# Joining the first layer's feature tiles in threes, with the block's order written out by hand

## The chip, the cores and the metric

The kernel runs on one core of a Trainium2 chip. The metric is the device time of one execution in microseconds (us), the median of several runs. A profile of one execution gives the time of each instruction on the engines: TensorE (PE, its weight loads shown apart as PEld), VectorE (DVE), ScalarE (ACT), GpSimd (POOL) and SyncE (SP), which here issues the transfers.

## What is computed

An RWKV6 attention (4 sequences, 8 heads of 48 dimensions, 768 tokens) feeds a two-layer network on 3072 tokens:

```python
for t in range(S):                                   # attention, per sequence and head
    cur = np.einsum('bhd,bhe->bhde', u[None] * kt, vt)
    y[:, :, t] = np.einsum('bhd,bhde->bhe', rt, state + cur)
    state = wt[:, :, :, None] * state + np.einsum('bhd,bhe->bhde', kt, vt)
...
h = x @ w_in                 # x: 3072 x 384 (the attention's results), w_in: 384 x 2048
g = h - np.tanh(h)
return g @ w_out             # w_out: 2048 x 384
```

## The kernel before

The tokens are worked on in 8 blocks of 384 (two for each sequence). A block's x lies transposed in three tiles of 128 x 384 (`xT`), and the 2048 features are 16 tiles of 128. For each feature tile there are four steps:

- the first layer: h = w_in x into PSUM, either plain (`first`, L899: three products of 128 x 384 columns) or joined (below);
- `slight` (L977), which makes g: on ACT two tanh of h with different scales and a square (L987, L988, L991), on DVE a product of the two results (L905). These three activations are called a slot below;
- forms of g: the second layer of a pair of tiles is done with 15 products of 128 x 128 in place of 18 for each 128 tokens (`Fewer`, L1082). It needs ten sums and differences of parts of g, made two at a time by `form_g` (L1006, DVE, 128 x 256 each, five per pair). Some forms read the one made just before;
- the products (L1096): twelve go into three PSUM accumulators (`acc`), three "odd" ones into `hp`. At the end of a block, twelve sums on DVE (`sum`, L1124 and L1132) turn the 15 accumulated results into the output, which goes out from `sums`.

The joined first layer of blocks 2 to 7 is `Twos` (L911): two feature tiles by 11 products of 192 columns (half of the block's tokens, L961) in place of 12. Weight forms (`kept`) are made once (L937); four token forms for each block (`turned`, L945) are differences of parts of x. One ACT copy (L962) and four additions on DVE (L971) for a pair make h in `joint`. In block 2 three of the eight pairs are joined, in blocks 3 to 6 six, in block 7 seven; the other tiles are plain.

Beside this runs the attention of the next block. For each block and half of the heads there are, in this order: running products of the decays (L431, L443), their products with k and r (L450, L457), splitting into 16-bit parts and transposing (ACT copies L556 and L566), scores of earlier tokens on PE (L508) with masked copies out of PSUM on DVE (`earlier`, L516), the state update on PE (L589) and DVE (L601), the results (`together`, L785) and ACT's copies of them into xT (L757), and a bound on the size of exponents (`bound`, L474, ACT, 128 x 780).

Each engine works through its instructions in the order in which the program wrote them. For the work around a tile f the program writes: the first layer's products, `slight`, then the list `ops` on DVE (the product of the tile before, forms, attention work, sums, mixed one by one by `between`), then what `due` says of the second layer's products, some tiles later. `plan(i)` says at which tile each piece of the attention stands. `EMPTY` counts empty instructions strewn between PE's products.

Of the kernel before, what the change touches and what calls it, by code (L numbers as in the profile page):

```python
# [37 lines left out]
F32 = mybir.dt.float32  # L38
# [81 lines left out]
TWOS = range(7)  # L120
BESIDE = (0, 1, 2, 3, 4, 7)
EMPTY = (159, 0, 92, 0, 16, 0, 40, 0)
JOINED = {2: (1, 4, 7), 3: BESIDE, 4: BESIDE, 5: BESIDE, 6: BESIDE, 7: TWOS}
PAIRS = range(0, 1), range(1, 2), range(2, 3), range(3, 5), range(7, 8)
LEFT = range(5, 7)
FORMED = {(1, 8): (1, (0, 2, 1, 4, 3)), (2, 5): (4, (0, 2, 1, 4, 3)), (2, 6): (3, (0, 2, 1, 4, 3)),
          (2, 12): (0, (0, 2, 1, 4, 3)), (2, 13): (2, (0, 2, 1, 4, 3)),
          (6, 12): (5, (0, 2)), (6, 13): (5, (1, 4, 3))}
# [8 lines left out]
def kernel(  # L137
# [59 lines left out]
    def draw(names, cols):  # L197
        nc.gpsimd.memset(mask_all[0:L, cols], 1.0)
        for m in names:
# [5 lines left out]
            else:  # L205
# [13 lines left out]
    states = [states0[:, 0:NPAIR * NCH * L].rearrange("d (p c e) -> d p c e", c=NCH, e=L),  # L219
              const.tile([P, NPAIR, NCH, L], F32, name="states1", tag="states1")]  # L220
# [13 lines left out]
    def g_at(q, x):  # L234
        if not isinstance(x, str):
            return 6 + q % 2 * 4 + x if x < 4 else 10 + x
        return (q % 2 * 3 if x[1] == "a" else 20 + q % 4 * 3) + int(x[0])

# [40 lines left out]

    class Kept:  # L280

        def __init__(self, pool):
            self.both, self.n = [pool.tile([P, 2, BANK], F32, name=f"att{j}", tag=f"att{j}") for j in range(2)], 0

        def tile(self, *_, **__):
            self.n += 1
            return self.both[self.n % 2]

    class Turns:
# [4 lines left out]
        def tile(self, *_, **__):  # L296
            self.n += 1
            return self.tiles[(self.n - 1) % len(self.tiles)]
# [8 lines left out]
    def scratch(ps):  # L307
        return ps.tile([P, 2, BANK], F32, name="att", tag="att")
# [19 lines left out]
    kept = const.tile([P, 5 * len(BESIDE) * P], F32, name="kept", tag="kept")  # L328
    turned = const.tile([P, 2 * NB], F32, name="turned", tag="turned")
    joint = const.tile([P, 6 * HB], F32, name="joint", tag="joint")  # L330
# [3 lines left out]
    class Block:  # L334
# [87 lines left out]
        def begin(self):  # L422
            self.xT = [xpool.tile([P, NB], F32, name=f"xT{i}", tag=f"xT{i}") for i in range(KC)]
            self.late = None
            return self.xT
# [62 lines left out]
        def gram(self, ps, lhs, rhs, p0, n, m=None, spare=0, ahead=0, late=0):  # L488
# [7 lines left out]
            used = ps_t[:, :, 0:n * NCP * width]  # L496
            gr = used.rearrange("s h (p c t) -> s h p c t", p=n, c=NCP)
            for p in range(p0, p0 + n):
                for c in range(NCP):
                    for h in range(2):  # L500
                        for par in range(2):
                            rows = slice(64 * h, 64 * h + D)
                            src = self.chunk(rhs, p, 2 * c + par, rhs == "pre" and not m)[rows]
                            dst = gr[64 * par:64 * par + 64, h, p - p0, c, :]
                            if m:
# [3 lines left out]
                                                         start=True, stop=True)  # L509
                            self.opened = self.opened or self.done  # L510
            return used

        def masked(self, ps, lhs, rhs, mask, p0, **fill):
            gr = self.gram(ps, lhs, rhs, p0, UP, **fill)
            mask = mask.bitcast(U8).unsqueeze(1).unsqueeze(1)
            return lambda x=0, n=UP: nc.vector.copy_predicated(  # L516
                out=A[:, :, p0 + x:p0 + x + n].rearrange("s h p c t -> s h (p c) t"),
                mask=mask.to_broadcast([P, 2, n * NCP, L]),
                data=gr[:, :, x * NCP * L:(x + n) * NCP * L].rearrange("s h (n t) -> s h n t", t=L))
# [15 lines left out]
        def turn_2(self, p0):  # L535
            ks = self.keys()[:, p0:p0 + UP]
            nc.scalar.copy(out=ks.rearrange("t p c d -> t p (c d)"), in_=self.turned_as[:, :, 0:NCP * P])
# [35 lines left out]
        def update_1(self, ps):  # L573
            last, wide = self.q == NQ - 1, D if isinstance(ps, Kept) else L
            for cs in ((0, 1), (2,)):
                kvp = scratch(ps)
# [3 lines left out]
                for p in reversed(range(NPAIR)):  # L580
                    for c in cs:
                        for h in range(2):
                            for par in range(2):
                                if last and 2 * c + par == NCH - 1:
# [6 lines left out]
                                                 rhs=self.v[toks, c, e0:e0 + D], start=True, stop=True)  # L591

        def update_2(self):
# [9 lines left out]
            if self.q > 0:  # L603
                step(St[:, :, 0, 0:D], St[:, :, 0, 0:D], tot(0), ALU.mult)
            for c in range(NCH - 1 if self.q == NQ - 1 else NCH):
                dst = St[:, :, c + 1, 0:D] if c + 1 < NCH else states[self.q + 1][:, :, 0, 0:D]
                kv = self.kv[c].rearrange("d (p e) -> d p e", e=D)
# [138 lines left out]
        def result_out(self, pairs, copy=None):  # L746

            copies = []
            for p in reversed(pairs):
# [3 lines left out]
                src = self.yp[p % 2][:, :, n * NCP * L:(n + 1) * NCP * L].rearrange("e a (c t) -> e c a t", t=L)  # L753
                dst = self.xT[p] if p < KC else self.late
                dst = dst.rearrange("e (c a t) -> e c a t", a=2, t=L)
                for h, rows in enumerate((slice(0, D), slice(64, 64 + D)) if copy else (slice(0, P),)):
                    copies.append((copy[h] if copy else nc.scalar.copy)(out=dst[rows], in_=src[rows]))  # L757
            return copies[0]

        def together(self, ps):  # L760
# [34 lines left out]
            for of in (from_state, scores) if self.q else (scores, from_state):  # L795
                for cross in range(2):
                    stretch(of, cross)
            self.result_out(ALL, None if spread else [nc.scalar.copy] * 2)
# [9 lines left out]
        def phase(self, ps, name):  # L808

            if name in ("own", "earlier"):  # L810
# [41 lines left out]
        def level(self, ps, m, p0, n):  # L852
            gr = self.gram(ps, "post", "pre", p0, n, m)
# [54 lines left out]
    def spare_tile(name, width=2 * HALF, pool=inp):  # L908
        return pool.tile([P, width], F32, name=name, tag=name, bufs=1)

    class Twos:  # L911
# [3 lines left out]
        def __init__(self):  # L915
            self.forms, self.sets, self.to = {}, [], []

        def form(self, pairs, tiles):
            tiles = [t.rearrange("p (j c) -> p j c", c=P) for t in tiles]
            self.sets.append((pairs, tiles))  # L920
            for n, j in enumerate(pairs):
# [696 lines left out]
```

## Time and profile before

| | |
|---|---|
| median of 3 runs | 537.41 us (536.76 to 539.31) |
| the profiled execution | 535.64 us |
| its span, first to last instruction | 533.9 us |
| granted TensorE clock | 0.999 |
| busy time of PE, DVE, ACT | 523.9, 478.1, 312.4 us |
| first token form of blocks 2, 4, 5, 7 | 152.5, 276.5, 339.2, 463.9 us |

Shares of the span are busy shares: PE 98%, DVE 90%, ACT 59%. Lines such as L961 are lines of the kernel before; those of the changed kernel are other numbers. In the profile's rows stand the start, the duration, the engine, the line, the operation, the tile written and the tiles read, the shape and the number of instructions in the row; the time in brackets is how long the engine had been idle, with what ended that. "128x384" is 128 partitions by 384 columns.

### The profile page before, as it was taken

How to read it: one execution, taken by the hardware profiler on the slowest of the kernel's cores; microseconds unless marked ns; L12 is line 12 of the kernel's file. 1: busy time of each engine (PE TensorE's matmuls, PEld its weight loads, DVE VectorE, ACT ScalarE, POOL GpSimd, SP SyncE). 2: the span in 40 equal slices, each digit the busy share in tenths (PEclk: the TensorE clock that was granted, in tenths of full speed). 3: DMA queues.
4: the chain of work that ended last, by engine and by line, in shares of the span. 5: the costliest groups of instructions: out<-in, count | busy, mean ns of one | idle time of the engine just before them, and what ended most of it. 6: DMA issues, size and time to landing. Idle time of an engine off the chain costs nothing.

```text
span 533.9 us, 14969 instructions
## 1 busy us (share of the span) xinstructions
PE 523.9 (98%) x6040; PEld 449.2 (84%) x6040; DVE 478.1 (90%) x1011; ACT 312.4 (59%) x729; POOL 9.1 (2%) x57
## 2 busy tenths in 40 slices
PE   7999999999999999999999999999999999999996
PEld 5756665677887879999799998999889997999994
DVE  7999996698889999999999999999999999667874
ACT  4999984665536473655646375375735655454350
POOL 1100000000000000000000000000000000000001
PEclk9999999999999999999999999999999999999999
DMA  8799632352312452035420832145321430200011
GB/s 282 258 406 342 224 120 71 107 132 64 122 26 72 104 143 95 0 89 166 120 58 2 192 119 66 54 66 142 108 88 31 79 116 1 58 1 1 10 36 48
DMA packets 53048, 56.35 MB, mean 106 GB/s; under 512 B 21488, under 2 KB 50928, under 8 KB 52976
## 3 DMA queue, kind: packets, MB, share of 16 engines
q1 hardware_dynamic: 52592, 55.18, 34.7%
q8 instruction: 49, 0.80, 0.6%
q14 instruction: 23, 0.19, 0.1%
q10 hardware_dynamic: 288, 0.10, 0.1%
q0 software_dynamic: 96, 0.07, 0.1%
HBM read 44.73 MB, written 4.72 MB: 93 GB/s over the span
## 4 chain that ended last, share of the span: by engine, by line
PE 83%; DVE 13%; issue 2%; DMA 1%; SPq 0%; DVEq 0%
PE acc L1096 23%; PE att L961 20%; PE hp L899 17%; PE acc L1047 6%; PE hp L1096 5%; PE att L785 3%; DVE g L1010 2%; PE att L508 2%; DVE joint L971 2%; DVE g L905 1%; PE att L589 1%; DVE pre L431 1%; PE acc L1074 1%; PE att L1096 1%; PE att L899 1%
## 5 line engine op out<-in xcount | busy, mean ns | idle before, releaser
L1096 PE MATMUL acc<-forms,g 128*128 128x128 f32 x972 | 135.5, 276 | 0.0
L1096 PEld LDWEIGHTS acc<-forms,g 128*128 128x128 f32 x972 | 124.3, 192 | 3.8
L899 PE MATMUL hp<-xT,w_sb 128*128 128x384 f32 x330 | 116.5, 489 | 0.0
L1010 DVE TENSOR_TENSOR g<-g 128x256 f32<-128x256 f32 x270 | 110.5, 418 | 6.1 <-DVE g L1010 0.5
L899 PEld LDWEIGHTS hp<-xT,w_sb 128*128 128x128 f32 x330 | 59.5, 190 | 33.3
L905 DVE SCALAR_TENSOR_TENSOR g<-h,qa 128x384 f32<-128x384 f32 x112 | 61.7, 551 | 18.1 <-ACT h L991 17.9
L987 ACT ACTIVATE h<-joint 128x384 f32<-128x384 f32 x54 | 27.9, 517 | 77.5 <-DVE joint L971 77.5
L961 PE MATMUL att<-xT,w_sb 128*128 128x192 f32 x340 | 72.0, 326 | 0.0
L987 ACT ACTIVATE h<-hp 128x384 f32<-128x384 f32 x55 | 27.2, 495 | 58.5 <-PE hp L899 58.4
L991 ACT ACTIVATE h<-h 128x384 f32<-128x384 f32 x113 | 58.2, 515 | 0.0
L961 PEld LDWEIGHTS att<-xT,w_sb 128*128 128x128 f32 x340 | 56.4, 190 | 0.0
L971 DVE TENSOR_TENSOR joint<-joint,att 128x384 f32<-128x384 f32 (+1 forms) x108 | 51.6, 499 | 4.9 <-PE att L961 3.0
L1096 PE MATMUL acc<-w_sb,g 128*128 128x128 f32 x324 | 54.5, 277 | 0.0
L1096 PEld LDWEIGHTS acc<-w_sb,g 128*128 128x128 f32 x324 | 45.9, 192 | 4.4
L961 PE MATMUL att<-turned,kept 128*128 128x192 f32 x192 | 36.5, 327 | 0.1
L1132 DVE TENSOR_TENSOR sums<-sums 128x256 f32<-128x256 f32 x84 | 33.3, 410 | 1.4 <-ACT sums L1109 0.9
L1047 PE MATMUL acc<-w_sb,sums 128*128 128x384 f32 x96 | 33.7, 487 | 0.0
L272 ACT ACTIVATE up<-raw 128x768 f16<-128x768 f32 (+1 forms) x32 | 33.0, 1108 | 0.0
L961 PEld LDWEIGHTS att<-turned,kept 128*128 128x128 f32 x192 | 32.0, 190 | 0.4 <-DVE turned L945 0.4
L1096 PE MATMUL hp<-w_sb,g 128*128 128x128 f32 x176 | 29.5, 275 | 0.0
L1047 PEld LDWEIGHTS acc<-w_sb,sums 128*128 128x128 f32 x96 | 18.1, 190 | 12.3
L988 ACT ACTIVATE qa<-joint 128x384 f32<-128x384 f32 x54 | 27.5, 509 | 0.0
(157 smaller groups left out, 795.5 us busy)
## 6 DMA issues: line engine op xcount, KB each, us to landing
raw<-in_weights SPq DMA_DIRECT2D x16, 768.0 KB, 7.4
w<-in_wT SPq DMA_DIRECT2D x7, 780.0 KB, 4.4
k<-in_kT SPq DMA_DIRECT2D x7, 768.0 KB, 4.6
r<-in_rT SPq DMA_DIRECT2D x7, 768.0 KB, 4.5
v_sb<-in_v SPq DMA_DIRECT2D x8, 576.0 KB, 5.1
k<-in_tokens SPq DMA_DIRECT2D x7, 576.0 KB, 4.1
r<-in_tokens SPq DMA_DIRECT2D x7, 576.0 KB, 4.2
out_y<-sums SPq DMA_DIRECT2D x18, 128.0 KB, 1.9
```

Source lines behind the costliest of these rows:

```text
L272: return lambda: nc.scalar.activation(out=to, in_=of, func=AF.Copy, scale=scale, bias=bias)
L899: nc.tensor.matmul(hp, lhsT=w_in_sb[:, f, kc, :], rhs=xT[kc], start=(kc == KC - 1), stop=(kc == 0))
L905: return lambda: nc.vector.scalar_tensor_tensor(out=out, in0=in0, scalar=scalar, in1=in1, op0=op0, op1=ALU.mult)
L961: nc.tensor.matmul(to, lhsT=lhs, rhs=rhs, start=n == 0, stop=n + 1 == len(of))
L971: return [lambda of=of: nc.vector.tensor_tensor(out=of[0], in0=of[1], in1=of[2], op=ALU.add) for of in ((h[:, 0:5:4], twice(h[:, 3]), both ...
L987: made = nc.scalar.activation(out=t, in_=h, func=AF.Tanh, scale=INNER / UPSCALE)
L988: nc.scalar.activation(out=by, in_=h, func=AF.Tanh, scale=OUTER / UPSCALE)
L991: nc.scalar.activation(out=t, in_=t, func=AF.Square, accum_out=top[:, n:n + 1])
L1010: return lambda: nc.vector.tensor_tensor(out=G[:, to:to + 2], in0=two(G, g_at(q, a0), g_at(q, a1)), in1=two(G, g_at(q, b0), g_at(q, b1)), ...
L1047: nc.tensor.matmul(acc, lhsT=g[:, j * P:(j + 1) * P], rhs=w_out_sb[:, f, :], start=(f == self.first), stop=(f == NF - 1))
L1096: nc.tensor.matmul(to, lhsT=G[:, g_at(q, a), :], rhs=rhs, start=start, stop=stop, skip_group_check=True)
L1132: ops.append(lambda op=op, at=at: nc.vector.tensor_tensor(out=at[0], in0=at[1], in1=at[2], op=OPS[op]))
```

## The change

`Twos` becomes `Threes` (L961 of the changed kernel): in blocks 2 to 7 three feature tiles are made by 15 products of 192 columns in place of 18, in five triples (tiles 0 to 2, 3 to 5, 6 to 8, 10 to 12, 13 to 15); tile 9 (`LONE`) is plain, and in block 7 so are tiles 13 to 15. Two sets of running sums lie in four PSUM banks, and some sums are to be used at two stages. So the products stop at stages where ACT copies a sum out with its sign changed (a "tap", L1047: three between the stages and at the end, four of 384 columns and one of 192 for each triple), into SBUF or into another bank where the next products are added. After the last tap six additions on DVE (L1050) give h of three tiles.

```diff
+        def begin(self, banks, f0, between, fill):
...
+            products((3, sums[0]), (5, sums[1]), start=3)
+            between(0)
+            tap(both(1), both(0, True))
+            products((0, singles[0]), (12, singles[1]), start=0)
+            fill(0)
+            products((2, chain[0]), (11, chain[1]))
+            between(1)
+            tap(T[:, 3:7:3], both(1))
+            products((8, sums[0]), (14, sums[1]), (13, apart_sums[0]), start=13)
+            fill(1)
+            products((10, chain[0]), (7, chain[1]))
+            between(2)
+            tap(T[:, 5], apart_sums[0])
+            tap(T[:, 0:5:4], both(1))
+            products((9, apart_sums[1]), (4, apart_sums[0]))
+            fill(2)
+            products((6, chain[0]), (1, chain[1]))
+            tap(T[:, 1:3], both(1))
+            between(3)
+            adding(T[:, 4:7], T[:, 1:4], T[:, 4:7], "add")
+            adding(T[:, 1], singles[0], T[:, 1], "sub")
+            adding(T[:, 0:3:2], both(0), T[:, 0:3:2], "add")
+            adding(T[:, 4:7:2], both(2), T[:, 4:7:2], "sub")
+            adding(T[:, 5], T[:, 5], T[:, 1], "sub")
+            adding(T[:, 1], singles[1], T[:, 1], "add")
```

`between(n)` writes at stage n the slot of a tile of the triple before and lists for ACT and DVE (A, V), `fill(n)` gives PE second-layer products. Eleven of the fifteen products use weight forms, in all 55 tiles of 128 columns: too many to keep. They are made in blocks 0 and 1 (17 operations on 384 columns for three triples, 17 on 256 for two; L993, L994), written to memory (`drawn`), and read back for each triple in three parts into one area (`ring`, 11 x 128 columns, 720 KB). The token forms of a block are six operations (L1016: four of 384 columns, two of 192).

The order of blocks 2 to 7 is written out by hand: a period for each triple, with the pieces of the attention, the forms, sums and loads at fixed places.

```diff
+        def between_stages(n):
+            if n < 3:
+                if waiting:
+                    ins, ops = slot(n)
+                    made.append(ins)
+                else:
+                    ops = []
+                run(A[n])
+                run(V[n] + ops)
+            else:
+                run(A[3])
+        def fill(n):
+            pull((3, 1, 2)[n])
+            run(fills[n])
+        threes.begin(banks, TRIPLES[t], between_stages, fill)
...
+        period(2, [form(fewer, 0, 1), form(fewer, 1, 0) + sums_of[:4], sums_of[4:] + form(fewer, 1, 1),
+                   form(fewer, 2, 0) + of(later, "diagonal_in 2", "diagonal_in 0")],
+               [[], [lambda: phase("join 0 0")], [lambda: phase("join 0 1")], [lambda: phase("join 0 2")]],
+               [[], [], [lambda: odd(fewer, 0)]], tail_2)
+        h = first(blk.xT, LONE, banks[1][:, 0:NB])
+        chain = later.update_2(True) if later else []
+        waiting.insert(0, (i, LONE, h))
+        made, ops = slot(0)
+        run(form(fewer, 2, 1) + chain[:2] + ops)
+        pull(6)
+        def tail_3(made):
+            load(after, "r", made)
+            pull(6)
+            odd(fewer, 2)
+            if later:
+                ps_a.n = 0
+                later.together(ps_a, None)
+                later.result_by_bank()
+                later.fill_holes([nc.sync])
...
+        period(4, [form(fewer, 4, 0), of(after, "behind 0", "take_whole 0") + form(fewer, 4, 1), of(after, "before 2"),
+                   form(fewer, 5, 0) + [lambda: run(threes.token_forms(later.x))]],
+               [[], [lambda: after and after.bound(HALVES[0])], [lambda: after and after.bound(HALVES[1])], []],
+               [[], [], [lambda: odd(fewer, 3)]], tail_4)
```

`pull(n)` writes the next n of the second layer's products (L1198) that are due; `odd` writes a pair's three odd products, which now add up over all eight pairs, so that the sum of two halves (L1124) goes. Also changed: the state update is copied out of PSUM by ACT (`update_out`, five copies), the results go out in eight copies of 192 columns by PSUM bank (`result_by_bank`, L807), masked copies of 768 columns become two of 384, g has 41 tiles of room in place of 32, and `EMPTY` is 275 in place of 307.

The order on DVE in a middle block before, around the additions of a pair (L971), with the forms L1010:

```order
L971 TENSOR_TENSOR joint<-joint,att_128 128x2x192
L1010 TENSOR_TENSOR g<-g 128x256
L971 TENSOR_TENSOR joint<-joint,att_127 128x2x192
L971 TENSOR_TENSOR joint<-joint,att_127 128x192
L971 TENSOR_TENSOR joint<-joint,att_127 128x384
L457 TENSOR_TENSOR post<-k,post 128x768
L1010 TENSOR_TENSOR g<-g 128x256
L457 TENSOR_TENSOR post<-k,post 128x768
L1010 TENSOR_TENSOR g<-g 128x256
L450 TENSOR_TENSOR pre<-r,pre 128x12x64
L1010 TENSOR_TENSOR g<-g 128x256
```

and on DVE now, in period 0, with the token forms L1016, the forms L1112 and the products L1098:

```order
L1016 TENSOR_TENSOR area<-xT 128x384
L1016 TENSOR_TENSOR area<-area,xT 128x384 x2
L1016 TENSOR_TENSOR area<-xT,area 128x384
L1016 TENSOR_TENSOR area<-xT,area 128x192
L1016 TENSOR_TENSOR area<-area 128x192
L1112 TENSOR_TENSOR g<-g 128x256 x3
L467 TENSOR_TENSOR post<-k,post 128x768
L460 TENSOR_TENSOR pre<-r,pre 128x12x64
L1098 TENSOR_TENSOR g<-h,qa 128x384
L1112 TENSOR_TENSOR g<-g 128x256 x2
L440 RECIPROCAL start<-whole 128x12
L441 SCALAR_TENSOR_TENSOR pre<-w,start 128x780
```

The forms that stood singly between other work now stand in twos and threes. On PE before, the products of a pair and those of the second layer behind it:

```order
L961 MATMUL att_128<-xT_1894,w_sb 128x192
L961 MATMUL att_128<-xT_1895,w_sb 128x192
L961 MATMUL att_128<-xT_1896,w_sb 128x192
L961 MATMUL att_128<-turned,kept 128x192
L961 MATMUL att_127<-turned,kept 128x192 x2
L961 MATMUL att_127<-xT_1896,w_sb 128x192
L961 MATMUL att_127<-xT_1895,kept 128x192
L961 MATMUL att_127<-xT_1896,kept 128x192
L961 MATMUL att_127<-turned,w_sb 128x192
L961 MATMUL att_127<-xT_1896,w_sb 128x192
L1096 MATMUL acc_133<-forms,g 128x128 x4
```

and on PE now, most of a triple in period 3 (the banks att_598 to att_601):

```order
L1028 MATMUL att_598<-area,w_sb 128x192
L1028 MATMUL att_598<-area 128x192
L1028 MATMUL att_601<-area,w_sb 128x192
L1028 MATMUL att_601<-xT,area 128x192
L1198 MATMUL acc_126<-forms,g 128x128 x2
L1198 MATMUL acc_596<-w_sb,g 128x128
L1028 MATMUL att_599<-area,w_sb 128x192
L1028 MATMUL att_599<-area 128x192
L1028 MATMUL att_598<-xT,area 128x192 x2
L1028 MATMUL att_600<-xT,area 128x192
L1198 MATMUL acc_596<-forms,g 128x128
L1028 MATMUL att_599<-area 128x192 x2
```

The products of a triple stand in pairs with the second layer's between them. On ACT before, the results' copies (L757) with the slots around them:

```order
L987 ACTIVATE h<-hp 128x384
L988 ACTIVATE qa<-hp 128x384
L991 ACTIVATE h,top<-h 128x384
L757 COPY outward_118<-att_128 128x384
L757 COPY xT_1315<-att_127 128x384
L757 COPY xT_1314<-att_128 128x384
L757 COPY xT_1313<-att_127 128x384
L987 ACTIVATE h<-hp 128x384
```

and on ACT now, from period 3 to period 4, with the copies L807, the slots L1088 and L1093, and the first tap L1047:

```order
L807 COPY xT<-att_598 128x3x64 x2
L807 COPY xT<-att_599 128x3x64 x2
L807 COPY outward_118<-att_600 128x3x64
L807 COPY xT<-att_600 128x3x64
L807 COPY outward_118<-att_601 128x3x64
L807 COPY xT<-att_601 128x3x64
L1088 ACTIVATE h<-area 128x384
L1088 ACTIVATE qa<-area 128x384
L1093 ACTIVATE h,top<-h 128x384
L1047 ACTIVATE att_599<-att_598 128x384
L1088 ACTIVATE h<-area 128x384
```

The copies stand ahead of the first slot, and the tap that the products wait for stands behind it.

607 lines of the change are left out of this document (369 added, 238 removed).

## The prediction

> **What bounds the kernel now.** I read the page first (busy line, share of the chain, waits), then the windows from one start of a block's token forms to the next, then the chain inside a middle block, then the rows of VectorE (DVE) and ScalarE (ACT) for prices. The page's busy line, its chain by engine, and from the waits of DVE the largest:
>
> ```profile
> PE 523.9 (98%) x6040; PEld 449.2 (84%) x6040; DVE 478.1 (90%) x1011; ACT 312.4 (59%) x729; POOL 9.1 (2%) x57
> PE 83%; DVE 13%; issue 2%; DMA 1%; SPq 0%; DVEq 0%
> DVE g L905 <- ACT h L991: 17.9, 18, 2.0
> ```
>
> TensorE (PE) carries the end, but DVE is busy 90% of the time. By block this is sharper. The windows are: start-up and blocks 0 and 1, two middle blocks, the last block; after the length come the busy times of PE, its weight loads, DVE, ACT, POOL, then the granted clock and the DMA share.
>
> ```profile
> 0.00:152.52 152.52, 148.55 (x1818) 103.33 (x1819) 132.69 (x247) 109.96 (x209) 5.49 (x33) 1.00 0.55 187
> 276.48:339.19 62.71, 62.71 (x767) 58.62 (x767) 60.37 (x129) 35.76 (x92) 0.32 (x4) 1.00 0.36 92
> 339.19:401.50 62.31, 62.31 (x766) 58.27 (x765) 60.12 (x129) 35.74 (x92) 0.32 (x4) 1.00 0.37 93
> 463.87:533.90 70.03, 65.35 (x456) 60.78 (x455) 50.29 (x128) 29.33 (x82) 2.17 (x6) 0.99 0.07 21
> ```
>
> A middle block takes 62.3 us, PE has no idle time in it, and DVE only 2.2 us. So PE bounds it by a hair: what is taken from PE can shorten a block by about 2 us, unless DVE's work shrinks too. The change does the opposite.
>
> [...]
>
> The chain, for PE's prices (an entry counts weight loads and matmuls, so x22 is 11 products):
>
> ```profile
> 291.65 1.74 PE att L508 x96
> ...
> 294.93 3.58 PE att L961 x22
> 298.50 2.68 PE acc L1096 x24
> ...
> 318.39 1.43 PE att L589 x80
> ...
> 321.35 1.94 PE hp L899 x6
> ...
> 327.90 2.83 PE att L785 x192
> ...
> 525.63 2.62 PE acc L1074 x8
> ```
>
> Hence 3.58/11 = 0.326 us for a product of 192 columns, 2.68/12 = 0.2235 for one of 128 columns in the second layer, 1.94/3 = 0.646 for one of 384 columns in the first; 1.74 for the scores of the earlier tokens, 1.43 for the state updates, 2.83 for the attention's results.
>
> DVE's rows:
>
> ```profile
> 344.92 0.55 DVE L971 TENSOR_TENSOR joint<-joint,att 128x384 f32<-128x384 f32 x1
> 345.39 0.42 DVE L1010 TENSOR_TENSOR g<-g 128x256 f32<-128x256 f32 x1
> 345.72 1.40 DVE L971 TENSOR_TENSOR joint<-joint,att 128x384 f32<-128x384 f32 x3
> 347.04 0.95 DVE L457 TENSOR_TENSOR post<-k,post 128x768 f32<-128x768 f32 x1
> 347.91 0.42 DVE L1010 TENSOR_TENSOR g<-g 128x256 f32<-128x256 f32 x1
> ...
> 355.23 1.97 DVE L516 COPY_PREDICATED scores<-mask_all,att 128x768 f32<-128x768 uint8 x2
> 357.09 0.41 DVE L1010 TENSOR_TENSOR g<-g 128x256 f32<-128x256 f32 x1
> ...
> 364.51 1.48 DVE L1010 TENSOR_TENSOR g<-g 128x256 f32<-128x256 f32 x3
> 365.91 0.55 DVE L905 SCALAR_TENSOR_TENSOR g<-h,qa 128x384 f32<-128x384 f32 x1
> ```
>
> Durations overlap, so I count from start to start: 0.47 us for 384 columns (344.92 to 345.39), 0.33 for 256 (345.39 to 345.72), 0.87 for 768, and by that slope 0.27 for 192 and 0.67 for 576. Two masked copies of 768 take 1.86, thus about 0.5 for half of one. The last pair matters most: three second-layer forms (L1010) in a row, each reading the one before, take 1.40 (364.51 to 365.91), where three that stand apart take 3 x 0.33 = 1.0. A form right behind the form that it reads costs about 0.2 more, and I take 0.12 (an operation that waits for one thing) to 0.19 (for two).
>
> ACT's rows:
>
> ```profile
> 338.84 0.52 ACT L987 ACTIVATE h<-joint 128x384 f32<-128x384 f32 x1 [2.98 <-DVE joint L971]
> ...
> 340.19 0.51 ACT L987 ACTIVATE h<-joint 128x384 f32<-128x384 f32 x1
> ...
> 382.85 0.94 ACT L474 ACTIVATE outward<-w,shift 128x780 bf16<-128x780 f32 x1
> ...
> 383.91 0.95 ACT L474 ACTIVATE outward<-w,shift 128x780 bf16<-128x780 f32 x1
> ...
> 393.14 0.48 ACT L757 COPY outward<-att 128x384 f32<-128x384 f32 x1 [2.74 <-PE att L785]
> 393.52 1.25 ACT L757 COPY xT<-att 128x384 f32<-128x384 f32 x3
> ```
>
> The three activations of a tile (a slot) take 1.35 us from start to start, a bound 1.06, a copy of 384 columns 0.38 (0.48 until its data is there).
>
> **The change part by part.** *PE.* 57 first-layer products of 384 columns and 374 of 192 go, 435 of 192 come: -57 x 0.646 + 61 x 0.326 = -16.9 us, that is 2.9 in each of blocks 3 to 6. The second layer's products stay. If PE alone counted, the profiled execution's 535.6 would become 518.7.
>
> *DVE.* A middle block's additions go from 24 operations to 30 (five triples by 0.67 + 3 x 0.27 + 2 x 0.47 = 2.4 us): 10.0 to 12.0 us; the token forms from 4 x 0.27 to 4 x 0.47 + 2 x 0.27: +1.35; the masked copies cut in two +0.2; the sum of the odd products, 0.47, goes. That is +3.1. The new order puts the forms in twos and threes right behind each other and the twelve sums in runs: 24 operations wait for the one in front instead of 12, and at 0.12 to 0.19 the bubbles grow from 3.6 to 6.5 us. Together +5.9 on the 60.1 to 60.4 above, so about 66.5 us of DVE work in a block of 62.3. This cannot be hidden: at best (PE and ACT always in time) a middle block grows by some 4 to 5 us. Blocks 0 and 1 get 34 weight forms for the ring, net +12.2 us of DVE, in a window with 19.8 us of DVE idle. Bounds: 0, if all of it fits, and 12.2, if none does. I take 2.5: eleven of the added operations (0.47 each, 5.2) stand ahead of the masked copy of the diagonal scores in block 0, and about half of that reaches PE. So 155.0 to the first token forms.
>
> *The loop of a triple.* Before, a pair's 11 products ran without a wait, and ACT and DVE followed with a pair of PE work in between. Now the products stop at each of the four taps on ACT, and ACT has the slots of the tiles before in the same line, whose first needs the adds just done. From the start of slot 0: three slots 4.05, the two taps between them 0.75, the small tap 0.32, a product 0.33, the fill in front of the last two products (two pulled and three odd ones, 5 x 0.2235 = 1.12), those two 0.65, about 0.3 for hand-overs, the last tap 0.48: 8.0. Then six adds, 2.4 + 2 x 0.12 = 2.6. So 10.6 us at least for each period, when DVE has nothing else; what ACT or PE must do in between comes on top. For a middle block, from the end of one period's adds to the next:
> - period 0: DVE's own work rules (token forms, four products of 768, a scan, ten forms): 16.4;
> - period 1: PE has the scores (1.74) and the odd products (0.67) ahead, then DVE must copy two banks out (1.0) before products may write there. What is left of this after the adds, 1.75, delays the first tap: 12.4;
> - period 2: DVE's work, with twelve sums: 13.3, and 0.3 for waits: 13.6;
> - period 3 with the lone tile 9: PE does 18 pulled products (4.02), the update (1.43) and the tile (1.94), of which 3.3 lie beside the tap and the adds before. The lone slot starts at about 3.6 or 4.1 and takes 1.35, then the loop: 3.6 + 1.35 + 8.0 + 2.6 = 15.5;
> - period 4: a pulled product reads a form that DVE makes only after the adds; then the odd products 0.67 and the results 2.83 end near 4.4, and the eight copies on ACT (at least 8 x 0.19 = 1.5, at most 8 x 0.38 = 3.0; part beside PE) near 6.05. They stand ahead of slot 0, and two bounds (2.1) stand among the slots: 6.05 + 8.0 + 2.1 + 2.6 = 18.8.
>
> These are 76.7 us for 62.3, and DVE is idle 10 of them. Block 2 (no slots in its first period) is about 75, block 6 (no bounds) 74.5. Block 7: period 0 waits for forms and token forms (2.5): 13.1; then 10.6, 12.3, 14.7; its tail has 24 us of PE work (three plain tiles 5.8, 36 pulled products 8.0, nine odd 2.0, four tiles added directly, priced as plain ones, 7.8), less 3.3 beside the last adds, plus 5.7 from the last row of the chain (525.63 + 2.62) to 533.9, plus 2 for slots: 28. That is 78.7 for 70.0.
>
> Sum: 155.0 + 75 + 3 x 76.7 + 74.5 + 78.7 = 613.3 of span. The profiled execution was 535.64 with a span of 533.9, so 1.7 lies around it: **615 us**. The median shown, 537.41, is 0.3% above the profiled one; I leave that out.
>
> *Loads.* About 27 reloads of 720 KB in three parts on SP's queue, some 20 MB. Before, a middle block used 0.37 of the DMA engines; five reloads add 3.6 MB to the 93 GB/s x 62.3 us = 5.8 MB of a block, thus about 0.5 over the longer block. I cost them at nothing: each part is issued once its products are done and has most of a period (10 us) to land. If that cover is gone, product 5, the second of a triple, is late first. Bounds: 0, and 30 periods x 2 us = 60.
>
> **Rivals.** *B: DVE is the bound with few waits.* If the loop is shorter than I make it (PE is idle some 17 us of a block, so no engine but DVE is near full), blocks 2 to 7 take DVE's work (381 us at these prices) and the 20 us idle of the last block, plus 1 us per block: 152.5 + 381 + 20 + 6 = 559.5, +1.7 = 561; with half of my waits 588. For it: DVE has 60 of 62 us before. Against: ACT's single line.
> *C: faster.* PE stays the bound and gives 518.7 to 535. This holds only if DVE's additions cost under 2.2 us a block, that is if neither the bubbles nor the wider token forms and adds cost what the rows say. Against it: 364.51 to 365.91.
> *D: slower still.* The ring's parts come late, or PE's rate falls in its new idle gaps; the longest, before the first products of period 0, is 3.6 us, because they need the token forms. If in each of six blocks 3.6 us of PE work took twice its time, that would be 6 x 3.6 = 22: 637. The trace grants 1.00 throughout, but has no such gap after the start.
>
> [...]
>
> **How the numbers follow.** A, the loop as written (601 to 632), 0.62; B (553 to 600) 0.24; D (over 632) 0.09; C 0.05. The range 572 to 636 takes in A, the upper half of B and the start of D, about 0.8. A difference of 0.5% (2.7 us) is about what a measurement of this kernel can tell from none. Only C can be faster, 0.04, or the same, 0.01; slower 0.95.
>
> **What would show it.** In the changed profile: PE's busy time falls by about 17 us and its share below 85%; DVE's busy time rises to some 520; starts of the token forms 72 to 78 us apart; DVE's largest waits at the first add (for ACT's tap) and at the product (for ACT's square), PE's at the products behind a tap; in period 4 ACT's first slot starts some 6 us after the last add. I am wrong if DVE is busy over 95% of a middle block (B), if PE has no idle time (C), if PE waits for the ring's loads, or if the clock in the windows falls below 1.00 (D).

## The result, and the profile after

The changed kernel takes 665.4 us (median of 4 runs, 661.2 to 666.4) against 537.1 us before: 1.236 times as long, with an interval of 1.230 to 1.243. The forecast was 615 us, with a range up to 636. Slower was right, the size was not: 128 us were lost where 78 were forecast. The profiled execution took 664.5 us, with a span of 662.6.

The page after: busy line, chain by engine, and the granted clock in 40 slices (tenths).

```profile
PE 560.0 (85%) x6048; PEld 478.7 (72%) x6048; DVE 518.4 (78%) x1074; ACT 364.8 (55%) x887; POOL 9.1 (1%) x57
PE 44%; DVE 28%; ACT 19%; issue 5%; DMA 2%; SPq 1%; PEld 0%; DVEq 0%; POOL 0%; POOLq 0%; PEldq 0%; ACTq 0%
PEclk9899999999999889998799987999878998899998
```

No engine is near full any more. The chain passes between PE, DVE and ACT, where before it was 83% PE. DVE's busy time is the forecast's (some 520). PE's has grown by 36 us, although its products would cost 17 us less at the old rate. One reason is the clock line, which now drops several times a block and before was 9 throughout (mean granted clock 0.945, before 0.999).

Two windows, from one start of the token forms to the next (block 4, and block 7 with the end):

```profile
324.59:409.82 85.23, 69.28 (x764) 64.04 (x764) 65.87 (x139) 44.81 (x118) 0.32 (x4) 0.92 0.40 110
574.27:662.60 88.33, 71.41 (x454) 63.29 (x454) 53.19 (x130) 35.78 (x99) 2.15 (x6) 0.94 0.14 39
```

Block 4 takes 85.2 us with 65.9 us of DVE work (66.5 forecast). So DVE is idle for 19 us of it, in place of the 10 forecast. The waits show for whom (engine, tile and line, then what it waited for: total, times, longest):

```profile
ACT area L1047 <- PE att L1028: 87.2, 40, 4.6
DVE area L1050 <- ACT area L1047: 57.5, 18, 6.1
DVE g L1098 <- ACT h L1093: 46.2, 30, 7.0
PE att L1028 <- ACT area L1047: 33.8, 36, 2.6
PE att L1028 <- DVE area L1016: 22.9, 6, 3.9
PE acc L1198 <- DVE g L1112: 18.4, 7, 2.9
ACT outward L484 <- DMA xT<-outward: 7.5, 4, 1.9
```

The first four are the loop: the tap on ACT waits for PE's products, the additions and PE's next products wait for the tap, and DVE's product waits for ACT's square. The next two, for the token forms and for a form of g, are waits that the forecast named too. The last one it had not seen: a bound on ACT waits for a transfer.

A period's length is read from DVE's rows, from the end of the last of its six additions (L1050) to the same of the triple after. In us:

| | period 0 | 1 | 2 | 3 | 4 | sum |
|---|---|---|---|---|---|---|
| forecast, middle block | 16.4 | 12.4 | 13.6 | 15.5 | 18.8 | 76.7 |
| changed kernel, block 4 | 16.8 | 13.3 | 14.0 | 16.4 | 24.9 | 85.2 |

Four periods are within 1 us of the forecast. Period 4 is 6 us off, in each of blocks 2 to 5. In block 4 the additions before it end at 384.25 (383.89 + 0.36), and then stand these rows of ACT:

```profile
383.89 0.36 DVE L1050 TENSOR_TENSOR area<-att,area 128x192 f32<-128x192 f32 x1
```

```profile
389.81 1.22 ACT L807 COPY xT<-att 128x192 f32<-128x192 f32 x4 [8.40 <-PE att L835]
...
391.76 0.58 ACT L1088 ACTIVATE h<-area 128x384 f32<-128x384 f32 x1
...
396.88 0.94 ACT L484 ACTIVATE outward<-w,shift 128x780 bf16<-128x780 f32 x1 [1.91 <-DMA xT<-outward]
...
405.77 0.49 ACT L1047 ACTIVATE area<-att 128x384 f32<-128x384 f32 x1 [4.63 <-PE att L1028]
```

Slot 0 starts 7.5 us after the additions (forecast 6.05). Then the bound waits 1.9 us: it writes a scratch result into `outward[1]`, out of which the results' last rows are still being moved to xT. And the last tap waits 4.6 us for PE. PE's rows say why, and also why slot 0 is late:

```profile
384.64 0.93 PE L1198 MATMUL acc<-forms,g 128*128 128x128 f32 x4 [2.86 <-DVE g L1112]
...
386.77 2.31 PE L835 MATMUL att<-pre,states 48*48 48x64 f32 x96
388.91 1.51 PE L835 MATMUL att<-scores,v_sb 64*48 64x64 f32 x96
...
398.35 1.40 PE L1028 MATMUL att<-area 128*128 128x192 f32 x4 [2.55 <-ACT area L1047]
...
403.11 0.64 PE L1198 MATMUL hp<-w_sb,g 128*128 128x128 f32 x2
403.54 0.63 PE L1198 MATMUL hp<-forms,g 128*128 128x128 f32 x2
```

From 403.11 to 403.54 one product of 128 columns takes 0.43 us (two entries each), and before it took 0.2235. PE runs at half rate, behind a gap of 2.55 us. So it does from 384.98 to 388.40 (granted clock 0.50), behind the gap of 2.86 us, where the results start. Five windows of 3.41 us, from just before the gap of 2.55 us, each with one granted clock (the third number from the end):

```profile
395.22:398.64 3.42, 0.87 (x7) 0.68 (x6) 3.21 (x8) 1.76 (x5) 0.00 (x0) 1.00 0.25 72
398.64:402.05 3.41, 2.33 (x8) 1.83 (x8) 1.41 (x2) 2.50 (x8) 0.00 (x0) 0.50 0.29 82
402.05:405.46 3.41, 3.41 (x16) 3.41 (x15) 0.00 (x0) 0.00 (x0) 0.00 (x0) 0.50 0.00 0
405.46:408.88 3.42, 2.96 (x26) 2.76 (x24) 2.44 (x6) 0.49 (x1) 0.00 (x0) 1.00 0.25 77
408.88:412.29 3.41, 0.00 (x0) 0.00 (x0) 3.13 (x8) 1.44 (x4) 0.00 (x0) 1.00 0.00 0
```

PE is busy 0.87 of 3.42 us, and the next window is granted 0.50. In that one PE is busy 2.33 us and the half clock stays. In the third it is busy throughout, and the fourth has the full clock again. The fifth, where PE waits for the token forms (busy 0.00), is followed by one at 0.50 once more. In a middle block four of 25 windows are at half clock.

### The profile page after: what moved, and what is told of

Same layout as the page of the kernel before. It is cut to its first block, busy times and chain, and to the rows that moved or that the text cites. A ratio compares the mean times of both kernels' runs of the same rounds, so it can differ in the third digit from the quotient of the medians.

```text
span 662.6 us, 15366 instructions
## 1 busy us (share of the span) xinstructions
PE 560.0 (85%) x6048; PEld 478.7 (72%) x6048; DVE 518.4 (78%) x1074; ACT 364.8 (55%) x887; POOL 9.1 (1%) x57
## 4 chain that ended last, share of the span: by engine, by line
PE 44%; DVE 28%; ACT 19%; issue 5%; DMA 2%; SPq 1%; PEld 0%; DVEq 0%; POOL 0%; POOLq 0%; PEldq 0%; ACTq 0%
PE acc L1198 10%; PE att L1028 8%; DVE area L1050 8%; PE hp L952 6%; ACT h L1093 5%; PE hp L1198 4%; DVE g L1112 4%; ACT h L1088 4%; PE att L952 4%; PE att L835 3%; PE acc L1149 3%; ACT area L1047 3%; DVE area L1016 2%; ACT qa L1088 2%; DVE scores L533 2%
## 5 line engine op out<-in xcount | busy, mean ns | idle before, releaser
L1198 PE MATMUL acc<-forms,g 128*128 128x128 f32 x972 | 141.7, 280 | 18.4 <-DVE g L1112 18.4
L1198 PEld LDWEIGHTS acc<-forms,g 128*128 128x128 f32 x972 | 131.8, 196 | 23.7 <-DVE g L1112 18.3
L1112 DVE TENSOR_TENSOR g<-g 128x256 f32<-128x256 f32 x270 | 112.6, 422 | 9.6
L1098 DVE TENSOR_TENSOR g<-h,qa 128x384 f32<-128x384 f32 x112 | 61.9, 553 | 46.7 <-ACT h L1093 46.2
L1028 PE MATMUL att<-area 128*128 128x192 f32 x348 | 88.5, 353 | 11.0 <-ACT area L1047 11.0
L1047 ACT ACTIVATE area<-att 128x384 f32<-128x384 f32 x116 | 48.5, 444 | 87.4 <-PE att L1028 87.2
L1028 PE MATMUL att<-area,w_sb 128*128 128x192 f32 x232 | 66.0, 369 | 31.3 <-DVE area L1016 22.9
L1028 PE MATMUL att<-xT,area 128*128 128x192 f32 x290 | 68.3, 352 | 22.7 <-ACT area L1047 22.7
L1050 DVE TENSOR_TENSOR area<-area 128x576 f32<-128x576 f32 (+1 forms) x58 | 32.1, 553 | 57.5 <-ACT area L1047 57.5
L1028 PEld LDWEIGHTS att<-xT,area 128*128 128x128 f32 x290 | 50.9, 200 | 32.2 <-ACT area L1047 32.1
L1028 PEld LDWEIGHTS att<-area 128*128 128x128 f32 x348 | 62.6, 205 | 13.1 <-ACT area L1047 12.6
L1088 ACT ACTIVATE h<-area 128x384 f32<-128x384 f32 x87 | 45.4, 522 | 26.7 <-DVE area L1050 22.2
L1093 ACT ACTIVATE h<-h 128x384 f32<-128x384 f32 x113 | 58.7, 519 | 0.0
L1198 PE MATMUL acc<-w_sb,g 128*128 128x128 f32 x324 | 56.3, 284 | 2.8 <-ACT sums L1219 2.8
L952 PE MATMUL hp<-xT,w_sb 128*128 128x384 f32 x162 | 57.0, 488 | 0.0
L1198 PEld LDWEIGHTS acc<-w_sb,g 128*128 128x128 f32 x324 | 48.3, 199 | 5.1 <-ACT sums L1219 3.6
L1050 DVE TENSOR_TENSOR area<-att,area 128x192 f32<-128x192 f32 (+1 forms) x116 | 47.7, 453 | 4.0
L1088 ACT ACTIVATE qa<-area 128x384 f32<-128x384 f32 x87 | 45.1, 518 | 0.0
L1198 PE MATMUL hp<-w_sb,g 128*128 128x128 f32 x200 | 43.2, 303 | 0.0
L1198 PEld LDWEIGHTS hp<-w_sb,g 128*128 128x128 f32 x200 | 34.5, 217 | 0.3
```

Source lines behind the costliest of these rows:

```text
L952: nc.tensor.matmul(hp, lhsT=w_in_sb[:, f, kc, :], rhs=xT[kc], start=(kc == KC - 1), stop=(kc == 0))
L1028: nc.tensor.matmul(to, lhsT=lhs, rhs=rhs, start=start, stop=True, skip_group_check=True)
L1047: nc.scalar.activation(out=out, in_=of, func=AF.Copy, scale=-1.0)
L1050: nc.vector.tensor_tensor(out=out, in0=in0, in1=in1, op=OPS[op])
L1088: made, _ = (nc.scalar.activation(out=to if len(h.shape) == 2 else to.rearrange("p (n t) -> p n t", t=HB), in_=h, func=AF.Tanh, scale=scal ...
L1093: nc.scalar.activation(out=t, in_=t, func=AF.Square, accum_out=top[:, n:n + 1])
```

## The experiments

The theory after the result: the loop is about as forecast, and three things were left out: the transfer that the bound waits for, the half clock where it lies on the loop, and a later start of period 4. Rivals: DVE bounds the block after all; the reloads of the ring are late; the half clock costs nothing, since PE has idle time.

**The bounds write elsewhere.**

```diff
-            junk = outward[1].bitcast(BF16)[:, 0:UP * NCH * LP]
+            junk = outward[to].bitcast(BF16)[:, 0:UP * NCH * LP]     # to = 0 in period 4
```

> The bounds of period 4 write into the other outgoing buffer, so that they need not wait until the results' last rows have left the one they share with them. In the changed kernel's trace the first of them waits 1.9 us for that transfer, in each of blocks 2 to 5, with slot 2 and two taps behind it. Theory (three losses in period 4: this wait, TensorE's half clock, results behind pulled products): 1.9 us less in each of four blocks, and the idle gap of PE behind it shrinks from 2.5 to under 1 us, so that the half clock that follows there goes too, another 2 to 3 us each: 645 to 657 us in place of 665. Rival one (the clock is slow for another reason than the gap): 657. Rival two (DVE or the reloads of the ring bound the block): 663 to 666.

Measured: 650.6 us, clock 0.957. Period 4 falls from 24.9 to 20.5 to 20.7 us in three blocks and to 22.3 in the fourth; the other periods of blocks 2 to 5 stay within 0.1 us, but for one first period that grew by 0.9. So in those three blocks 1.9 us of wait carried another 2.3 us with it, as the theory expected of the half clock.

**PE kept busy in its gaps.**

```diff
+    def warm(n):
+        for _ in range(n):
+            nc.tensor.matmul(hp[:, NB:BANK], lhsT=w_in_sb[:, 0, 0], rhs=w_in_sb[:, 0, 1], start=False, ...)
...
+                warm(10)        # tail_3, before pull(6)
+               [[], [lambda: warm(8 if after else 0)], [lambda: odd(fewer, 3)]], tail_4)     # period 4
+            warm(12)            # tail_4, behind pull(12)
```

> Ten, eight and twelve idle products of 128 columns, whose results nobody reads, fill PE's three longest gaps of a block (2.9 us before the pulled products of period 3's end, 2.5 us in period 4, 3.9 us before period 0); at full clock they take 2.2, 1.8 and 2.7 us and fit in the gaps. Theory: no 3.4 us window is under half busy any more, the granted clock goes from 0.945 to 0.99 or more, and the time falls by what the half clock cost on the path: about 1 us in the results, 2.7 us in period 4's products, 3 to 4 us in block 7's first period, 635 to 648 us. Rival one (half clock costs nothing, since PE has idle time anyhow): 660 to 666 us with the clock up. Rival two (the clock does not depend on the gaps): clock at 0.945.

Measured: 652.1 us, clock 0.981, less of a gain than the theory gave (635 to 648 us, clock 0.99). Still, the idle products alone give 13 us back, without touching the work, so the half clock was on the path. It did not vanish: in block 4 the bound's wait for the transfer grew to 3.0 us, since everything ahead of it was earlier, and behind it PE still ran at half rate (0.42 us for a product of 128 columns).

**Both.** The first edit and the second together. The expectation speaks of idle products in two gaps, but the kernel that ran has them in all three, 142 as in the run before; the eight of period 4 in block 4 are this row:

```profile
381.75 1.95 PE L1567 MATMUL hp<-w_sb 128*128 128x128 f32 x16
```

> The changed kernel with the bounds in the other buffer and with idle products in the gaps before the pulled products of period 3's end and before period 0 (not in period 4's gap, which should be gone). Theory: without the transfer's wait and without half clock period 4 is the loop as the prediction summed it, 18.8 to 20 us in place of 24.9, and block 7's period 0 is 14.6; blocks 2 to 6 fall by 4.5 to 6 us each, 630 to 640. Rival (the two losses are one, since they overlap): 647 to 651, as with either edit alone.

Measured: 637.9 us, clock 0.992. Period 4 in block 4, ACT and then DVE, whose first and last row give the period's length (371.93 to 390.98):

```profile
377.88 0.58 ACT L1088 ACTIVATE h<-area 128x384 f32<-128x384 f32 x1
...
380.96 0.97 ACT L484 ACTIVATE outward<-w,shift 128x780 bf16<-128x780 f32 x1
...
387.64 0.49 ACT L1047 ACTIVATE area<-att 128x384 f32<-128x384 f32 x1 [2.39 <-PE att L1028]
```

```profile
371.57 0.36 DVE L1050 TENSOR_TENSOR area<-att,area 128x192 f32<-128x192 f32 x1
...
390.62 0.36 DVE L1050 TENSOR_TENSOR area<-att,area 128x192 f32<-128x192 f32 x1
```

Period 4 is 19.05 us (forecast 18.8). Slot 0 starts 5.95 us after the additions (6.05), and from there the last tap ends after 10.25 us (8.0 + 2.1). The two losses add up: 14.8 and 13.3 apart, 27.5 together. Whether period 4's gap needs no idle products once the wait is gone, this run does not show.

**The results first.** They stand ahead of the pulled and odd products at period 3's end.

```diff
-            pull(6)
-            odd(fewer, 2)
             if later:
...
                 later.fill_holes([nc.sync])
+            pull(6)
+            odd(fewer, 2)
```

> At the end of period 3 the attention's results and their copies stand ahead of the six pulled and three odd products, whose first waits 2.9 us for a form that DVE makes after its adds. Theory: the results start at once, their copies end some 5 to 6 us earlier, and slot 0 of period 4 starts about 1 us after the adds in place of 7.5: period 4 falls from 24.9 to 18 to 20 us, and blocks 2 to 6 each by 5 to 6.5 us: 632 to 642 us. Rival one (the products are needed as early, so that their delay costs as much elsewhere): 655 to 666. Rival two (DVE bounds period 4 with its own 13 us): no change beyond 2 us a block.

Measured: 656.5 us, in the range of the first rival. In blocks 2 to 5 period 4 takes 21.9 to 23.4 us, a fall of 1.3 to 3.0 where the theory gave 4.9 to 6.9. The first rival's reason holds only in part: the period behind grows by 0.9 us in block 5, and by 0.2 or less in blocks 3 and 4. The results' first row in period 4:

```profile
379.18 0.31 PE L835 MATMUL att<-pre,states 48*48 48x64 f32 x2 [2.30 <-DVE area L1050]
```

The results are written into the banks that the additions still read. Slot 0 starts 5.8 us after the additions in place of 7.5, and not 1. The expectation had overlooked the banks, and that the results, from 380.30 to 384.6 at half clock for the most part, would take 4.3 us and not 2.83 (the last 95 entries took 2.86 us, where 96 in the changed kernel took 1.51).

**The forms apart.** `mixed` takes from its lists in turn.

```diff
-            V = [form(last, 5, 1) + of(later, "times_behind 2", "times_before 2"), ...
+            V = [mixed(form(last, 5, 1), of(later, "times_behind 2", "times_before 2")), ...
```

> The forms, the twelve sums and the token forms stand alternately with other DVE work in place of in runs, so that fewer operations wait for the one just before. Theory: only periods 0 and 2 are bounded by DVE (16.8 and 13.9 us against 16.4 and 13.3 us of work), so only their bubbles count, 1 to 2 us a block: 653 to 660 us. Rival one (DVE bounds the whole block): 2.9 us in each of six blocks, below 650. Rival two (the bubbles lie beside waits for ACT everywhere): 663 to 666.

Measured: 660.0 us, 5.4 less, the least that was expected, but not where it was expected: in blocks 3 to 5 periods 0 and 1 fall by 0.3 and 0.1 us, period 2 by 0.2, and period 4 grows by 0.1 to 0.3, so that a block gains 0.4 at most in place of 1 to 2. Block 6's period 4 and block 7's first fall by 1.6 us each. Bubbles are a small part.

**Without the forms.** `form` makes none in blocks 2 to 7.

> Leaves out the making of the second layer's forms in blocks 2 to 7 (the products then read what lies there), 25 operations or 9 to 11 us of DVE with its bubbles in each block; all else stays. Theory (the serial loop of a triple over PE, ACT and DVE bounds periods 1, 3 and 4): only periods 0 and 2, which DVE bounds, fall, by 3 to 4 us each, and the wait for a form ahead of the results (up to 2.9 us) goes; a block falls from 85.3 to 74 to 78 us, the total to 605 to 625. Rival (DVE bounds the block): all periods fall with DVE's work, to 70 us or less a block, below 590.

Measured: 635.4 us, above the expectation. More DVE work went than was expected: a middle block has 40 forms and not 25, and in block 4 DVE's work is 50.9 us in place of 65.9:

```profile
315.17:396.14 80.97, 67.94 (x764) 63.07 (x764) 50.85 (x98) 44.84 (x117) 0.32 (x4) 0.94 0.42 116
```

So a middle block still takes 79 to 81 us without 15 us of DVE work, and period 0 still 16.2 to 16.3 in three blocks of four (14.5 in block 5). Its rows in block 4:

```profile
317.70 0.59 PE L1028 MATMUL att<-area,w_sb 128*128 128x192 f32 x2 [3.06 <-DVE area L1016]
...
319.88 1.49 PE L1198 MATMUL acc<-forms,g 128*128 128x128 f32 x6
```

So DVE does not bound the block, as rival B had it. Nor does DVE alone bound period 0, as the forecast had it: right under DVE's 16.4 us lies a second limit, the first products waiting for the token forms, and then running at half clock (1.49 us for three products).

**The reloads left out.**

```diff
-            if not (later is None and t == 3):
+            if i == JOINED and t == 0:
```

> The weight forms of the second triple are loaded once, in block 2, and not again: 28 of 29 reloads are left out, so that the products of other triples read the wrong forms. Theory (the reloads land in 2.4 to 2.7 us, long before they are needed; PE's waits are for ACT and DVE): 660 to 667. Rival (prediction's case D, late reloads or their contention with the other transfers): below 655.

By the trace 27 of 29 loads are left out, and not 28. With wrong weight forms the values were beyond the range that the short form of g allows for, and the kernel ran its slow general path behind the main part: 2757.7 us, which tells nothing. The main part is in the trace: its last triple's additions end at 629.2 us, against 628.8 in the changed kernel, and its block 4 from token forms to token forms:

```profile
325.94:411.34 85.40, 69.14 (x764) 63.81 (x764) 65.86 (x138) 44.83 (x118) 0.32 (x4) 0.92 0.27 68
```

85.4 us without the reloads and 85.2 with them: they cost nothing, as forecast. In the changed kernel they land soon after they are issued (KB each, us to landing):

```profile
area<-forms_of_w_in SPq DMA_DIRECT2D x58, 256.0 KB, 2.7
area<-forms_of_w_in SPq DMA_DIRECT2D x29, 192.0 KB, 2.4
```

**More DVE work in the kernel before.**

```diff
+            if 2 < i < 7 and f % 4:
+                spare.append(lambda x=here[f % KC]: nc.vector.tensor_reduce(out=more, in_=x, op=ALU.add, ...))
```

> The kernel before, with twelve more reductions of 384 columns on DVE (some 0.47 us each, 5.6 us a block) in each of blocks 3 to 6; their result is not used. The prediction's first step says that a middle block has only 2.2 us of idle DVE under its PE work (block 6: 5.7): three blocks grow by 3.4 us each and the fourth by up to 1, so 545 to 551 in place of 536.5. Rival (PE has slack in DVE's favour because its products are queued ahead): 536 to 540.

Measured: 550.2 us, 1.025 times the kernel before (1.022 to 1.027). Blocks 3 to 6 grow from 62.3, 62.7, 62.3, 62.4 to 66.0, 66.7, 66.5, 64.8 us (from one start of the token forms to the next). So the cover in blocks 3 to 5 is at most what the windows said, about 2 us (5.6 us added, 3.7 to 4.2 paid). Block 6 paid 2.4 us where at most 1 was expected. By this even a change with no loop and no waits, but with this one's 5.9 us of DVE a block, would lose; such a kernel was not run.

**The last fill behind the triple's last products.**

```diff
-            fill(2)
             products((6, chain[0]), (1, chain[1]))
             tap(T[:, 1:3], both(1))
+            fill(2)
```

> The changed kernel with the last fill of each triple (two pulled and three odd products, 1.12 us at full clock) written behind the triple's last two products in place of ahead of them. Theory: it lies on the serial loop of periods 1, 3 and 4, where the last tap and the adds wait for those two products, so 0.8 to 1.1 us go in each of those, twice that in period 4 at half clock, and 0 to 0.5 in periods 0 and 2, which DVE bounds: 3 to 4 us a block, 643 to 652. Rival (DVE's work bounds the block, or PE runs the fill in time that is idle anyway): 662 to 666.

Measured: 635.2 us, 30 less by moving one line, and more than the 13 to 22 that were expected. In blocks 3 to 5 periods 1 and 3 fall by 1.1 us each, just the 1.12 of the five products, and periods 0 and 2 do not fall: that is the serial loop by its own price. Period 4 falls by 3.5 us and block 7's first period by 2.0. What goes beyond the price there goes along with the granted clock (0.962 over the run in place of 0.945); no run separates the two.

**All edits, without and with the last fill moved.** The first two slots of period 4 go ahead of the results' copies too.

```diff
                 later.together(ps_a, None)
+                for _ in range(2):
+                    ins, ops = slot(0)
+                    run(ops)
+                    ahead.append(ins)
                 later.result_by_bank()
```

> The edits together: bounds in the other buffer, idle products before the results and before period 0, forms and sums apart, results ahead of the pulled products, and the first two slots of period 4 written on ACT ahead of the results' copies, for which ACT waits some 8 us. Theory: slots 0 and 1 leave the loop of period 4, which falls to 14 to 16.5 us, and periods 0, 2 lose 0.3 to 0.6: 600 to 618. Rival (DVE's own work of 66 us a block is near enough to bind as soon as the waits go): a block stays above 74 us, over 618.

Measured: 626.1 us, in the rival's range. Period 4 takes 16.9 to 18.6 us, longer than expected, and a middle block 76 to 77.5, as the rival has it. But DVE still waits for ACT, so DVE's work alone does not bind:

```profile
DVE area L1050 <- ACT area L1047: 52.3, 22, 3.9
DVE g L1098 <- ACT h L1093: 31.9, 28, 7.1
```

> The kernel with all edits together (626.1 us) and also the last fill of each triple behind the triple's last products. Theory: 0.8 to 1.1 us less in periods 1, 3 and 4 of six blocks, 0 to 0.3 in the others: 608 to 614. Rival (DVE, now with some 66 us of work in a block of 77, bounds what is left): 620 to 626.

Measured: 606.3 us, 20 us less again at nearly the same clock (0.992 in place of 0.988), a little more than expected, and 1.129 times the kernel before (1.126 to 1.132). With 69 us still lost, none of these versions beats the kernel before. In this one the periods are 15.4, 12.1, 13.3, 16.1, 17.4 us in block 4, 74.3 together, with 63.7 us of DVE work. What bounds this remainder was not tried.

## Why the prediction was right and wrong

- *What bounds, and the gain of 17 us.* Right: 2 us of cover in a block, and DVE's added work turns the change into a loss by itself (the run with more DVE work). DVE's busy time, 65.9 us in a middle block, was within 1 us. Wrong: PE's busy time does not fall by 17 us but grows by 36. The half clock, four of 25 windows of a block, is the larger part. Even in the run with both edits, at clock 0.992, PE's own products are busy for some 533 us, an estimate (565.1 on its page, less 142 idle products at 0.2235), against 524 before. The forecast took each product at its price in a long stream; whether the short groups make the difference was not tried.
- *The loop.* Right: 18.8 us of period 4 are 19.05 in block 4 (19.0 to 19.8 in blocks 2 to 5) once the two things below are gone; the fill's 1.12 us are 1.1 in the run that moves it. The rank of the waits that it named was also right.
- *Wrong, "period 4".* The prediction put the results at 2.83 us and then the loop at full rate, and read the bounds as two more pieces of 1.06 us on ACT. It did not ask what the bound writes. The buffer is shared with the results' way to xT, and the order by hand put them 3 us apart. Price: 1.9 us of wait in each of four blocks, and with the half clock that it set off, 14.8 us by the run that moves the bounds.
- *Wrong, "the longest gap is 3.6 us" and the chance of D.* The longest gap, before period 0, was 3.9 us and half clock followed it (0.50 from 412.29 in block 4), as D had it, but in blocks 3 to 6 that cost nothing: period 0 takes 16.8 us there with idle products and without, and only block 7's fell, from 17.0 to 14.6. The gaps that count were shorter, 2.9 us ahead of the results and 2.5 in period 4. With them four windows of a block are at half clock, and three of these lie in period 4, on the loop. The prediction held the clock for a rival of its own at 0.09, while its own case A, with 17 us of idle PE in a block, brings the gaps along with it, so that A and D were one case. Price: 13.3 us by the idle products alone.
- Half clock followed shorter gaps too: one of 2.55 us (PE busy 0.87 of the 3.42 us of its window), and in the run with the results first two of 1.8 and 1.6 us together (0.94 of 3.41). D's term, 6 x 3.6 us lost to the gap before period 0, no run shows: the runs show only the 2.4 us of block 7's first period.
- *The rest.* The span was 613.3 forecast and 662.6 measured. The two points above are 27.1 us of it (662.6 to 635.5 in the run with both edits). Of the other 22, blocks 3 to 5 take 9 us more than summed, most of it 0.9 us in each of periods 1 and 3, and block 6 another 4. No run tried where these 0.9 us come from, but the rows show two terms of the loop's sum that are too small. In period 1 of block 7, which was summed as the bare loop, the run with both edits takes 11.3 us in place of 10.6:

```profile
569.03 0.59 PE L1028 MATMUL att<-xT,area 128*128 128x192 f32 x2 [0.52 <-ACT area L1047]
569.46 0.49 PE L1028 MATMUL att<-area 128*128 128x192 f32 x2
569.78 0.61 PE L1198 MATMUL acc<-w_sb,g 128*128 128x128 f32 x4
```

Behind the small tap stand two products ahead of the fill, 0.75 us from 569.03 to 569.78, where the sum has one at 0.33; and from the end of the last tap the additions take 2.85 us in place of 2.6. Block 7 takes 7.6 more, 5.8 of which lie behind its last triple. There the twelve sums stand in one run behind the last check and DVE does them when PE is nearly done, so that the outputs come late:

```profile
650.17 0.15 DVE L1794 TENSOR_SCALAR again<-att 1x1 int32<-1x1 f32 x1 [1.28 <-PE att L1793]
650.25 4.99 DVE L1253 TENSOR_TENSOR sums<-sums 128x256 f32<-128x256 f32 x12
...
657.16 0.35 DVE L1180 SCALAR_TENSOR_TENSOR g<-att,g 128x192 f32<-128x192 f32 x1
```

That these sums are the cause of the late end is read from the rows; no run moved them. Blocks 0 and 1 ended at 155.4 us (155.0 forecast). Their 2.5 us for the weight forms stood between bounds of 0 and 12.2, so that much of this fit is luck.
- *Rival B* is refuted by the run without forms, *C* by the result itself, with its reason by the run with more DVE work, and the late reloads of *D* by the run without them.

## What to carry to other kernels

Before a saving on the bounding engine is counted, take the next engine's idle time in that stage from the windows: what the change adds there beyond it is paid, and here 2 us of cover met 6. When work that was queued ahead becomes a chain over three engines, sum the chain once round, each row at its price, and then look at two things that the sum itself makes: the buffers that its pieces share with transfers, and the idle gaps of TensorE, which here cost a second time through the clock (13.3 us). An instruction between the stages belongs behind the last one that somebody waits for.

## What the runs showed of the hardware that was not expected

Half clock followed gaps of PE that the forecast had counted as idle time alone: 2.55 us in period 4 of the changed kernel, where PE was busy for 0.87 us of a window and the next was granted 0.50 (the first two of the five windows further above).

It also followed two short gaps together, 1.8 and 1.6 us in the run with the results first:

```profile
391.68:395.09 3.41, 0.94 (x5) 0.65 (x5) 2.52 (x4) 3.41 (x11) 0.00 (x0) 1.00 0.28 73
395.09:398.50 3.41, 3.41 (x14) 3.41 (x15) 0.00 (x0) 0.30 (x1) 0.00 (x0) 0.50 0.06 21
```

In the changed kernel's trace the busier of two windows could have the slower clock behind it. A window at full clock with PE busy for 2.12 of 3.41 us (183.60 to 187.01) was followed by one at 1.00; the second of the five windows further above, at half clock with PE busy for 2.33, was followed by another at 0.50. So in this kernel a stage whose products come in short groups with waits between them stayed at half clock although PE was busy most of the time; the full clock was back behind the third window, with PE busy throughout (3.41 us).
